# Homes at multiples of 128 bytes for TensorE's operands

## The chip, the core and the metric

The kernel runs on one core of a Trainium2 chip. The metric is the device time of one execution in microseconds (us); the median of three runs of the kernel before is 1080.55 us (1077.29 to 1080.92). SBUF, the on-chip memory from which TensorE reads, has 128 partitions; a tile has the same start address, its home, in each of them. This document gives homes modulo 128 bytes.

## What is computed

Linear attention with an exponential feature map, then two gated MLPs, all in float32:

```python
def phi(x):                                   # x: 4 x 8 heads x 576 x 64
    proj = x @ w_phi                          # 64 -> 128
    proj = proj - max(abs(proj))
    return concat([exp(proj), exp(-proj)])    # 256 features
q_p, k_p = phi(q), phi(k)
kv, z = k_p.T @ v, sum(k_p)                   # per head
x = (q_p @ kv) / (q_p @ z + 1e-6)             # 2304 tokens x 512
x = (silu(x @ w_gate) * (x @ w_val)) @ w_out        # 512 -> 1536 -> 512
x = (sigmoid(x @ w_gate2) * (x @ w_val2)) @ w_out2
```

## The kernel before

**Attention** comes first (to about 190 us). `proj` (line 315) multiplies tiles of q and k by w_phi; every operand is split into a high and a low part (`xh`, `xl`, `w2h`, `w2l`) of type float32r, and three products stand for one. There the moving operand, which streams through the array, is w_phi with 256 columns and the stationary one, which is loaded before, is x with 128. `k_sum` (line 361) sums exp(k) times v; v lies in a tile of four heads with 66 columns each, 64 values and two ones. `turn` (line 383) transposes the subtracted projections of q (`sub`), and `ratio` (line 410) makes numerators and denominators, which go through DRAM; `den_load` (line 430) reads denominators back into a small tile of 18 columns to invert them.

**MLPs** follow. Four passes over the weights (two for each MLP, `hh` 0 to 3) each go over five blocks of tokens, four of 512 and one of 256, and in each over three slots of weights `w0`, `w1`, `w2`: a unit. `product` (line 606) makes the seven products of a Strassen scheme (four in the small block), each as 2 x 2 x 3 matmuls of 256 columns: x is the moving operand, the weights are the stationary one. A full unit has 84 such matmuls, one of the small block 48. ScalarE and VectorE sum and gate the results (lines 626 to 657), and `accumulate` (lines 676 and 678) multiplies by the output weights `o0`, `o1`, `o2`: in passes 0 and 1 the result u of the gate is the moving operand, in passes 2 and 3 the output weights are. Its matmuls are issued between the products of the next unit. While a pass runs, the weights of the next one are loaded, unpacked (lines 158 to 174), stored, loaded again and split (line 198).

**The order.** A planner gives each step a time (`at`), sorts them and issues them in that order; each engine works through its own list. SyncE issues all loads and stores.

**The homes.** Tiles of a pool lie side by side, each rounded up to 32 bytes. Pools on the left grow upwards from the constants: w0, w1 (with o0, o1), `stage`, x0, u, and then `aq` of attention, later replaced by x1. Pools on the right grow downwards from the top of the memory, byte 229344, which is 96 modulo 128: `ap`, `ak`, `ae` of attention, later replaced by w2 (with o2). The pools are opened in lines 111 to 116 and 776 to 777, and `swap` (line 780) replaces them.

Of the kernel before, what the change touches and what calls it, by code (L numbers as in the profile page):

```python
# [9 lines left out]
F32 = mybir.dt.float32  # L10
# [9 lines left out]
P = 128  # L20
# [8 lines left out]
XW = 256  # L29
HW = 512  # L30
VW = D + 2

LEAD = 5
EB = 2
# [70 lines left out]
def body(ctx: ExitStack, tc: tile.TileContext, qT, kT, v, w_phi2, wpk, out):  # L105
# [8 lines left out]
    stage = ctx.enter_context(tc.tile_pool(name="stage", bufs=1))  # L114
# [132 lines left out]
    def plan_attention(ap, ak, ae, aq, t0):  # L247
# [92 lines left out]
        kt, kv, kvz, v1s = {}, {}, {}, {}  # L340

        def load_v(i):
            qd, tt = divmod(i, NT)
            v1s[i] = ak.tile([P, 4, VW], F32, tag="v1", name="v1", bufs=4)
            nc.gpsimd.memset(v1s[i][:, :, D:], 1.0)
            nc.sync.dma_start(
                out=v1s[i][:, :, 0:D],
                in_=v[tt * P:(tt + 1) * P, qd * 256:(qd + 1) * 256]
                .rearrange("p (h d) -> p h d", h=4))

        def k_sum(i, b, r0, r1, first, last):
# [5 lines left out]
            for h in range(4):  # L357
                for s in range(2):
                    c = (h % 2) * 2 + s
                    for u in range(2):  # L360
                        nc.tensor.matmul(  # L361
                            kv[qd, b][h // 2][u * 64:(u + 1) * 64, c * P:c * P + VW],
                            e[r0:r1, h, s, u], v1s[i][r0:r1, h], start=first and c == 0,
                            stop=last and c == 3, skip_group_check=True)

        def kv_keep(qd, b, i):
            if i == 0:
                kvz[qd, b] = aq.tile([P, 4, 2, VW], F32, tag="z", name="z", bufs=2)
            ps = kv[qd, b][i].rearrange("p (h s m) -> p h s m", h=2, s=2)[:, :, :, :VW]
            nc.scalar.copy(kvz[qd, b][:, 2 * i:2 * i + 2], ps)  # L370
# [57 lines left out]
        dw = 4 * S // P  # L428

        def den_load(r, qd, b):  # L430
            r["d"] = stage.tile([P, dw], F32, tag="rc", name="rc", bufs=2)
            nc.sync.dma_start(out=r["d"], in_=den[b][4 * qd:4 * qd + 4]
                              .rearrange("h (p w) -> (h p) w", w=dw))

# [11 lines left out]
        for s, t in enumerate(step):  # L446
            i = s - LEAD
# [14 lines left out]
            if k < n:  # L462
                qd, tt = divmod(k, NT)
                if tt * P % XW == 0:
                    plan_x(kT, "k", qd, tt * P // XW, i)
                at(when(i, 1.5), load_v, k)
                kt[k] = {}
                plan_proj(pe(TP, lambda: None) - TP, kt[k], "k", qd, tt)
# [20 lines left out]
            for qd, g, hp in ratios:  # L489
                g0, m, b = GROUPS[g]  # L490
                e = pe(TR[m == 320], ratio, qd, g, hp)
                at(e + 0.1, ratio_out, qd, g, hp)
                ready["nd"] = e + 0.2
                at(e + 0.8, ratio_store, qd, g, hp)
                if hp == 2 and (g0 + m) % S == 0:
                    r = {}
                    at(e + 4.0, den_load, r, qd, b)
                    at(e + 7.0, den_inv, r)
                    at(e + 7.5, den_store, r, qd, b)
                    ready[b] = e + 7.5  # L500
# [272 lines left out]
    def pool(name, side="left"):  # L773
        return tc.tile_pool(name=name, bufs=1, side=side, reuse_waits="tile")

    aq, ap, ak, ae = pool("aq"), *(pool(name, "right") for name in ("ap", "ak", "ae"))
    aq_, *ap_ = (x.__enter__() for x in (aq, ap, ak, ae))
    T0, ready = plan_attention(*ap_, aq_, 0.0)
# [15 lines left out]
    for hh in range(4):  # L794
        begin.append(t)
        for j, (_, n) in enumerate(BLOCKS):
            if last:
                xprep.append((t, hh, j))
            for p in range(NPAIR):
                r = {}  # L800
# [76 lines left out]
```

## Time and profile before

| | |
|---|---|
| median of three runs | 1080.55 us |
| the profiled execution | 1078.06 us |
| its span, first to last instruction | 1076.0 us |
| granted TensorE clock, mean | 0.99 |
| instructions | 20722 |

The profile is of one execution. PE is TensorE's matmuls and PEld its weight loads, which run beside them; DVE is VectorE, ACT ScalarE, POOL GpSimd and SP SyncE. Matmuls overlap, so that the duration of one is longer than the step from its start to the start of the next; the step is called spacing here. A row names the line, the engine, the operation and the tiles, written one before the arrow; of a matmul's two operands the moving one stands first. Tiles of the same name in attention and in the MLPs (xh, xl, w2h, w2l) are told apart by the line: 315 is attention, 606 the MLPs.

### The profile page before, as it was taken

What the parts mean: (1) busy time and instruction counts of PE and PEld (TensorE: products, weight loads), DVE (VectorE), ACT (ScalarE), POOL (GpSimd) and SP (SyncE); (2) the same over time, 40 slices, a digit from 0 to 9 for tenths busy, and PEclk for the clock granted to TensorE, in tenths of its full rate; (3) what the DMA queues carried; (4) which work ended last, traced back from release to release, by engine and by line L of the source; (5) the groups of instructions that cost most, each with busy time, mean ns of one, the idle gap of its engine ahead of it and who ended that gap; (6) DMA issues with size and microseconds to landing.
All of it is one profiled execution on the core that took longest, in us unless ns stands there. A gap on an engine that the chain in (4) does not pass through costs nothing.

```text
span 1076.0 us, 20722 instructions
## 1 busy us (share of the span) xinstructions
PE 1034.5 (96%) x8344; PEld 928.7 (86%) x8344; DVE 745.5 (69%) x1274; ACT 558.1 (52%) x1006; POOL 126.1 (12%) x109
## 2 busy tenths in 40 slices
PE   7999999997999998999999989999999899999998
PEld 6777776786999888999998889999988799999997
DVE  6988888775766788667757886667487864463433
ACT  5888877643555555535444455455454553332322
POOL 3322330210000014100000132000001230000000
PEclk9999999998999999999999999999999999999999
DMA  7787766648755251445634524155434340331111
GB/s 216 213 243 216 237 190 222 210 117 241 232 172 170 94 187 50 148 136 182 220 120 140 183 99 157 64 190 168 130 97 158 98 147 11 117 119 40 40 40 40
DMA packets 88575, 157.41 MB, mean 146 GB/s; under 512 B 28896, under 2 KB 50592, under 8 KB 88480
## 3 DMA queue, kind: packets, MB, share of 16 engines
q1 hardware_dynamic: 88480, 156.10, 46.2%
q8 instruction: 65, 1.06, 0.4%
q14 instruction: 30, 0.25, 0.1%
HBM read 108.73 MB, written 47.33 MB: 145 GB/s over the span
## 4 chain that ended last, share of the span: by engine, by line
PE 74%; DVE 12%; DMA 8%; ACT 2%; issue 2%; SPq 1%; DVEq 0%; ACTq 0%
PE a L606 22%; PE b L606 16%; PE c L678 7%; PE c L676 5%; PE d L678 5%; PE d L676 5%; PE a L315 5%; PE d L410 4%; PE c L361 3%; DMA rb<-rden 3%; DMA raw<-wpk 2%; DVE xl L198 2%; DVE c L632 1%; PE b L383 1%; DMA o0l<-wfo 1%
## 5 line engine op out<-in xcount | busy, mean ns | idle before, releaser
L644 ACT ACTIVATE c<-c 128x256 f32<-128x256 f32 x96 | 50.4, 525 | 163.9 <-DVE c L632 163.8
L657 DVE TENSOR_TENSOR ul<-c,uh 128x512 fp32r<-128x512 f32 (+1 forms) x120 | 75.1, 635 | 49.5 <-ACT uh L656 48.9
L626 ACT COPY c<-a 128x512 f32<-128x512 f32 x96 | 56.1, 584 | 93.9 <-PE a L606 84.5
L632 DVE TENSOR_TENSOR c<-b,c 128x512 f32<-128x512 f32 x96 | 65.6, 683 | 53.5 <-PE b L606 48.7
L656 ACT CAST uh<-c 128x512 fp32r<-128x512 f32 (+1 forms) x120 | 68.5, 576 | 60.6 <-DVE c L649 52.6
L606 PE MATMUL a<-xh,w2h 128*128 128x256 f32 x288 | 83.1, 288 | 8.7 <-DVE c L632 8.7
L606 PE MATMUL a<-xh,w1h 128*128 128x256 f32 x288 | 81.2, 282 | 8.1 <-DVE c L632 8.1
L606 PE MATMUL a<-xh,w0h 128*128 128x256 f32 x288 | 80.9, 281 | 2.1 <-ACT c L626 1.6
L606 PE MATMUL a<-xh,w2l 128*128 128x256 f32 x288 | 82.6, 287 | 0.0
L606 PE MATMUL a<-xl,w2h 128*128 128x256 f32 x288 | 82.6, 287 | 0.0
L606 PE MATMUL a<-xl,w0h 128*128 128x256 f32 x288 | 80.6, 280 | 0.0
L606 PE MATMUL a<-xh,w1l 128*128 128x256 f32 x288 | 80.4, 279 | 0.0
L606 PE MATMUL a<-xh,w0l 128*128 128x256 f32 x288 | 80.4, 279 | 0.0
L606 PE MATMUL a<-xl,w1h 128*128 128x256 f32 x288 | 80.4, 279 | 0.0
L161 ACT ACTIVATE raw<-raw 128x512 int32<-128x512 uint32 x72 | 48.8, 680 | 60.5 <-DMA raw<-wpk 53.6
L649 DVE TENSOR_TENSOR c<-c 128x256 f32<-128x256 f32 x96 | 56.2, 585 | 27.7 <-ACT c L644 27.1
L198 POOL TENSOR_TENSOR w0l<-s,w0h 128x768 fp32r<-128x768 f32 x6 | 11.3, 1884 | 503.1 <-PE b L606 335.2
L165 DVE TENSOR_SCALAR wcv<-wcv 128x512 f32<-128x512 f32 x72 | 31.4, 437 | 54.6 <-ACT wcv L158 53.6
L606 PEld LDWEIGHTS a<-xh,w2h 128*128 128x128 f32 x288 | 55.4, 193 | 12.1 <-DVE c L632 10.0
L606 PEld LDWEIGHTS a<-xh,w1h 128*128 128x128 f32 x288 | 54.8, 190 | 12.5 <-DVE c L632 10.1
L606 PE MATMUL b<-xh,w2h 128*128 128x256 f32 x224 | 63.2, 282 | 0.0
L606 PE MATMUL b<-xh,w2l 128*128 128x256 f32 x224 | 63.0, 281 | 0.0
(181 smaller groups left out, 3497.4 us busy)
## 6 DMA issues: line engine op xcount, KB each, us to landing
raw<-wpk SPq DMA_DIRECT2D x72, 512.0 KB
b<-xo SPq DMA_DIRECT2D x32, 512.0 KB
wf<-wcv SPq DMA_DIRECT2D x48, 256.0 KB
a<-wf SPq DMA_DIRECT2D x24, 512.0 KB
part<-o SPq DMA_DIRECT2D x17, 512.0 KB
o<-part SPq DMA_DIRECT2D x17, 512.0 KB
wfo<-wcv SPq DMA_DIRECT2D x24, 256.0 KB
x<-kT SPq DMA_DIRECT2D x18, 256.0 KB
```

The costliest lines, as they stand in the source:

```text
L161: nc.scalar.activation(r["lo"].bitcast(I32), r["lo"], AF.Copy, scale=2.0 ** -29)
L315: nc.tensor.matmul(ps[:, i * 256:(i + 1) * 256], x[:, i, o:o + P], w, start=(m == 0 and i == 0), stop=(m == 2 and i == 1), skip_group_chec ...
L410: nc.tensor.matmul(pn[i * w:(i + 1) * w, :m], f, e[:, h, c, :m], start=(c == 0), stop=(c == 1))
L606: nc.tensor.matmul(o, f[:, c], x[:, c], start=k == first and w == 0 and c == 0 and m == 0, stop=c == 1 and m == 2, skip_group_check=True)
L626: anchor["act"] = nc.scalar.copy(part_of(r, d), parts(r, src))
L632: anchor["dve"] = nc.vector.tensor_tensor(out=c, in0=parts(r, "zy x"[d]), in1=c, op=ALU.add)
L644: nc.scalar.activation(o, g, AF.Silu if hh < 2 else AF.Sigmoid)
L649: nc.vector.tensor_tensor(out=o, in0=v, in1=places(r, j, 0, d)[1], op=ALU.mult)
L656: nc.scalar.copy(hi, v)
L657: nc.vector.tensor_tensor(out=lo, in0=v, in1=hi, op=ALU.subtract)
L676: nc.tensor.matmul(ps[:, :n], a[:, k], x, start=st, stop=sp)
L678: nc.tensor.matmul(ps, x[:, k], a, start=st, stop=sp)
```

## The change

Three edits. A tile of 96 bytes is opened first on the right and never used, so that everything on the right lies 96 bytes lower. The two tiles for denominators (`rc`) get 32 columns in place of 18, of which 18 are used; with 128 bytes in place of 96 each, what lies after them on the left moves up by 64. The tile of v gets 288 columns in place of 264, viewed as before.

| tiles | home before | home after |
|---|---|---|
| w0, w1, o0, o1 | 0 | 0 |
| x0, x1 (xh, xl), u (uh, ul) | 64 | 0 |
| w2, o2 | 96 | 0 |
| attention: x's parts, w_phi's parts, exp(k), sub | 96 | 0 |
| v, four buffers | 96, 64, 32, 0 | 0 |
| exp(q) | 64 | 0 |
| z, two buffers | 64, 0 | 0, 64 |

Inside v and z the heads stay 264 bytes apart.

```diff
+LINE = 32
...
         def load_v(i):
             qd, tt = divmod(i, NT)
-            v1s[i] = ak.tile([P, 4, VW], F32, tag="v1", name="v1", bufs=4)
+            v1s[i] = ak.tile([P, 9 * LINE], F32, tag="v1", name="v1", bufs=4)[:, :4 * VW] \
+                .rearrange("p (h d) -> p h d", h=4)
             nc.gpsimd.memset(v1s[i][:, :, D:], 1.0)
...
         def den_load(r, qd, b):
-            r["d"] = stage.tile([P, dw], F32, tag="rc", name="rc", bufs=2)
+            r["d"] = stage.tile([P, LINE], F32, tag="rc", name="rc", bufs=2)[:, :dw]
...
+    edge = ctx.enter_context(pool("edge", "right"))
+    edge.tile([P, 3 * LINE // 4], F32, name="edge")
     aq, ap, ak, ae = pool("aq"), *(pool(name, "right") for name in ("ap", "ak", "ae"))
```

## Rows read from the trace of the kernel before

**Rows 1.** The page: busy us of each engine, share of the span, instructions.

```profile
PE 1034.5 (96%) x8344; PEld 928.7 (86%) x8344; DVE 745.5 (69%) x1274; ACT 558.1 (52%) x1006; POOL 126.1 (12%) x109
```

**Rows 2.** Windows: length, busy us of each engine, granted clock, DMA share, GB/s.

```profile
50.00:100.00 50.00, 49.67 (x668) 38.02 (x667) 41.58 (x72) 40.50 (x85) 15.27 (x20) 1.00 0.79 231
...
186.00:295.00 109.00, 99.20 (x678) 87.95 (x679) 76.50 (x125) 54.41 (x94) 11.60 (x5) 0.95 0.65 199
295.00:412.00 117.00, 113.84 (x840) 106.79 (x840) 86.77 (x155) 64.66 (x111) 8.93 (x5) 1.00 0.46 149
```

**Rows 3.** Waits of TensorE: who for whom, us in total, times, longest.

```profile
PE a L606 <- DVE c L632: 17.3, 8, 3.2
```

**Rows 4.** Chain of waits, 295 to 320 us: start us, us, what.

```profile
306.08 2.72 PE b L606 x24
...
314.25 2.87 PE b L606 x24
```

**Rows 5.** Line 606: count, duration ns min/median/max, first and last start.

```profile
L606 PE MATMUL a<-xh,w1h x288: 276/276/415, 199.7 to 1050.5; 128*128 128x256 f32 x144
...
L606 PE MATMUL a<-xl,w2h x288: 278/282/415, 222.7 to 1064.8; 128*128 128x256 f32 x144
```

**Rows 6.** Chain of waits at the end of the first weight pass.

```profile
397.69 6.68 DMA o0l<-wfo
...
406.42 2.31 DVE xl L198
...
409.89 2.80 DVE w1l L198
...
417.13 2.92 PE a L606 x12
```

**Rows 7.** Timeline of matmuls in attention: start us, us, instruction.

```profile
76.09 0.28 PE L315 MATMUL a<-w2h,xh 128*128 128x256 f32 x1
...
76.69 0.28 PE L315 MATMUL a<-w2h,xl 128*128 128x256 f32 x1
```

**Rows 8.** Line 678 (passes 2 and 3), columns as in rows 5.

```profile
L678 PE MATMUL c<-o1h,uh x40: 388/390/494, 671.8 to 1063.0; 128*128 128x512 f32 x40
...
L678 PE MATMUL c<-o1h,ul x40: 388/392/502, 672.0 to 1063.2; 128*128 128x512 f32 x40
...
L678 PE MATMUL c<-o2h,uh x40: 392/399/402, 687.3 to 1070.0; 128*128 128x512 f32 x40
...
L678 PE MATMUL c<-o2h,ul x40: 392/399/400, 687.6 to 1070.2; 128*128 128x512 f32 x40
```

**Rows 9.** Line 676 (passes 0 and 1), columns as in rows 5.

```profile
L676 PE MATMUL c<-ul,o1h x40: 276/394/504, 225.9 to 627.3; 128*128 128x512 f32 x32, 128*128 128x256 f32 x8
```

**Rows 10.** Chain of waits, 725 to 755 us.

```profile
730.64 2.83 PE b L606 x24
...
741.88 2.83 PE b L606 x24
```

**Rows 11.** Groups of 420 to 610, then 860 to 1050 us: busy, mean ns.

```profile
L606 PE MATMUL b<-xl,w0h 128*128 128x256 f32 x56 | 15.5, 276 | 0.0
...
L606 PE MATMUL b<-xl,w0h 128*128 128x256 f32 x52 | 14.5, 279 | 0.0
```

**Rows 12.** Chain of waits: sums over two v buffers.

```profile
67.54 2.17 PE c L361 x64
...
111.66 2.17 PE c L361 x64
```

**Rows 13.** Groups of ScalarE, shapes apart: busy us, mean ns, idle before.

```profile
L197 ACT CAST w0h<-a 128x1024 fp32r<-128x1024 f32 x8 | 8.5, 1058 | 0.9 <-DVE a L216 0.9
...
L197 ACT CAST w2h<-a 128x1024 fp32r<-128x1024 f32 x8 | 8.4, 1050 | 0.3 <-DVE a L216 0.2
```

**Rows 14.** Timeline of weight loads in attention, columns as in rows 7.

```profile
76.09 0.19 PEld L315 LDWEIGHTS a<-w2l,xh 128*128 128x128 f32 x1
```

## The prediction

> **What bounds the kernel now.** I began with the busy times: TensorE is at 96% of the span, VectorE at 69%, ScalarE at 52% [rows 1]. Then the stages: from 50 to 100 us (attention) TensorE is busy for 49.67 of 50 us, and from 295 to 412 us for 113.84 of 117 us, which is the level of every later stage; only 186 to 295 us, where the first weights and activations of the MoE layers arrive, is at 91% [rows 2]. The waits of TensorE confirm it: the longest sum is 17.3 us in 8 waits, product's matmuls for VectorE's line 632 [rows 3]. So nearly every nanosecond between two matmuls counts, and the question is whether the homes of the operands set any of them.
>
> The change adds no instruction, DMA or wait: the edge tile is never touched, the values and denominators keep their shapes inside wider tiles, and every engine's program keeps its order. Only addresses move. So what has to be read is the spacing of matmuls by the home of their operands. I write "moving/stationary" for the two homes modulo 128 bytes: product (line 606) is 64/0 for w0 and w1 and 64/96 for w2; the projection (line 315) is 96/96; the output sums are 64/0 and 64/96 (line 676), 0/64 and 96/64 (line 678).
>
> Unbroken stretches of 24 products give the spacing best. 64/0 takes 2.72 us at 306 us, 113.3 ns each; 64/96 takes 2.87 us at 314 us, 119.6 ns each [rows 4]; the difference of 0.15 us is 6.25 ns a matmul. [...] The medians over the whole run say it again, 276 against 282 ns [rows 5]. The profile's duration holds some 163 ns beside the spacing (276 less 113), so differences of durations are differences of spacing.
>
> **The change part by part.** All terms are against the profiled execution, 1078.06 us (span 1076.0 and 2.06 around it).
>
> Edge tile, w2's products. Three groups (xh by w2h, xl by w2h, xh by w2l) of 288 and 224 make 1536 matmuls with weights from w2. If home 96 is what slows them and 0 gives w0's spacing, they save 1536 x 6.25 = 9.6 us. Not all of it is on the path. Near the end of each weight pass a chain of other work decides: the load of o0l (6.68 us), VectorE's splits (2.31 and 2.80 us) and the sum at line 632 fill 397.7 to 417.1 us before product goes on [rows 6]. A whole w2 unit (84 matmuls) lies under it, in three passes, and one more under the early waits of 186 to 295 us; there the gain only lengthens a wait. On the path remain 1536 - 4 x 84 = 1200, or 7.5 us. If home 96 costs nothing, the term is 0.
>
> Edge tile, projection. Both operands are at 96: from 76.09 to 76.69 us stand five spacings of 120 ns [rows 7]. 432 x (120 - 113.3) = 2.9 us; attention is bound by TensorE, and its end starts the normalisation for which the first MoE blocks wait, so the gain is kept. I count 2.6, leaving out the start, where DMA sets the pace; the lower end is 0 here too.
>
> Edge tile, w2's output weights. As the moving operand (line 678) o2 shows 399 and 399 ns where o1 shows 390 and 392 [rows 8]: 9 + 7 ns, each for 72 matmuls (40 into c and 32 into d), is 1.1 us. As the stationary one (line 676) I take 0, since its neighbour with o1 already stands at 394 ns [rows 9].
>
> Products of w0 and w1 in the second half. The 64/0 pair that took 2.72 us takes 2.83 us at 730 and 741 us, in units that follow w2 and o2 [rows 10], and the means of w0 rise from 276 to 279 ns [rows 11]. I found no operand that differs; the slower rhythm seems to be handed on by a misaligned neighbour. Taken at about 1.5 ns on the 1536 products of w0 and w1 in that half (w1's means rise less), 2.3 us is at stake; between 0 and 2.3 I take 1.5.
>
> Denominator tiles widened: x and u move from 64 to 0. This is the unknown term, since no row before has 0/0. The nearest rows are a pair that differs in which side is at 0: with 0/64 (o1 moving) a 512-column matmul lasts 390 and 392 ns, with 64/0 (o1 stationary) 394 ns as median [rows 8, 9]. A moving operand at 0 is no clear gain there, so I take 0. [...] The upper end is the third rival.
>
> Values padded. v's four homes were 96, 64, 32 and 0; two runs of 64 matmuls from different buffers take 2.17 us each [rows 12], so its own home costs nothing, and padding only brings the subtracted tiles below it to 0; they are stationary operands of the transposes, whose spacing no row shows at another home: 0. z's two buffers only swap their homes: 0. The writers of all moved tiles are nearest to ScalarE's casts, 1058 ns into w0 and 1050 into w2 [rows 13]: homes 0 and 96 alike, so 0.
>
> Sum: 7.5 + 2.6 + 1.1 + 1.5 = 12.7 us, 1078.06 - 12.7 = 1065.4 us. The median of the three runs is 1080.55, 2.5 above the profiled execution; from there it would be 1067.9. I put 1066, and 1060 to 1072 as this case's own range.
>
> **The rivals.**
> Even 64 costs, and 0/0 is faster than any row. [...] Against it: wide matmuls with a moving operand at 0 hardly stand below those at 64 [rows 8, 9]. [...]
>
> The home is not the cause. w2, the projection's tiles and o2 have in common that they lie at the high end of the memory, not only that they start at 96. If that place slows them, a shift by 96 bytes changes nothing: 1078 us. For it: nothing in the trace separates the two, and the homes of v make no difference [rows 12]. Against it: 96/96, 64/96 and 96/64 lie in different phases beside different neighbours, and all are slower. [...]
>
> Equal homes collide (slower). The next weight load begins with the current matmul: at 76.09 us both start [rows 7, 14]. If their reads disturb each other when both begin at the same place within 128 bytes, then 64/0 was the good arrangement, and the change makes all pairs equal. The only equal pair before, 96/96, takes 120 ns [rows 7]; at 6.25 ns the 3072 products of w0 and w1 lose 19.2 us, the wide matmuls of o0 and o1 go to o2's durations, 144 x 16 ns = 2.3 us, and w2 gains nothing: 1078 + 22 = 1100 us. It decides as soon as the equal start, and not the distance from a multiple of 128, is what counts. Against it: 64/96 and 96/64 are unequal and slow as well.
>
> **How the numbers follow.** Forecast 0.43, even lower 0.26, no effect 0.17, collision 0.14. Less than 0.5% (5.4 us) can't be told from no change here. The first two are faster, except for 0.02 in which the chains of the weight passes take most of the gain; no effect is the same but for 0.02 on either side. So faster 0.69, same 0.15, slower 0.16. The range goes from 1032, which takes in most of the lower rival, to 1082, no effect with the spread of the runs.
>
> **What would show it.** After the change 24 products of w2 should take 2.72 us and not 2.87, five projections 0.57 us and not 0.60, o2's matmuls 390 to 394 ns, and the stretches at 730 and 741 us 2.72 us. If w0 and w1 fall below 113 ns as well, the first rival holds; if w2 stays at 119, the second; if w0 rises to 119, the third. The waits for line 632 should grow by about 0.5 us in each of three weight passes. I'd be wrong in another way if the spacings fall as said and waits grow by as much.

## The result, and the profile after

The change makes the kernel slower. The median is 1089.75 us (1083.23 to 1092.42, 7 runs) against 1080.44 us (1075.84 to 1081.54, 7 runs), a ratio of 1.0085 with a 95% interval of 1.0062 to 1.0109. The forecast was 1066 and its range 1032 to 1082: wrong in sign. The rival in which equal homes collide names what happened.

The page of the kernel after, busy us of each engine, answers [rows 1]: VectorE and ScalarE are where they were, TensorE has 14.0 us more, nearly all that the span has gained (14.4, from 1076.0 to 1090.4). The granted clock is 0.990 and 0.992 in the mean of the two executions, so the clock is not the reason. The profiled execution of the kernel before (1078.06 us) lies 2.4 us below the median of its seven runs and that of the kernel after (1092.42) 2.7 above its own, so 14.4 us between the profiles stand for 9.3 between the medians.

```profile
PE 1048.5 (96%) x8344; PEld 945.0 (87%) x8344; DVE 747.4 (69%) x1274; ACT 558.9 (51%) x1006; POOL 127.2 (12%) x109
```

The chain of waits of the kernel after, 300 to 320 us (start, us, what), answers [rows 4]. The first row is 24 products of w1, the second of w2. Both take 2.88 us, 120.0 ns each: w2 was not brought down to w0 and w1, w0 and w1 were brought up to it.

```profile
308.17 2.88 PE b L609 x24
...
316.81 2.88 PE b L609 x24
```

The small block of pass 2, 725 to 765 us, answers [rows 10]. Here too there is now one spacing for all.

```profile
740.43 2.88 PE b L609 x24
...
751.67 2.88 PE b L609 x24
```

Line 609, which is line 606 of before, over the whole run (count, duration ns min/median/max), answers [rows 5]: 276 and 282 have become 283 and 283.

```profile
L609 PE MATMUL a<-xh,w1h x288: 277/283/415, 203.1 to 1065.0; 128*128 128x256 f32 x144
...
L609 PE MATMUL a<-xl,w2h x288: 282/283/420, 224.2 to 1079.4; 128*128 128x256 f32 x144
```

The projection in attention, timeline of matmuls, answers [rows 7]: from 77.50 to 78.10 us again five spacings of 120 ns. Moving both operands from 96 to 0 did nothing.

```profile
77.50 0.28 PE L317 MATMUL a<-w2l,xh 128*128 128x256 f32 x1
...
78.10 0.28 PE L317 MATMUL a<-w2h,xh 128*128 128x256 f32 x1
```

The output matmuls, line 681, answer [rows 8], and line 679 answers [rows 9]: o2 falls from 399 to 396 and 395 ns, but o1 rises from 390 and 392 to 396 and 397. With the stationary o1 in passes 0 and 1 the median is unchanged.

```profile
L681 PE MATMUL c<-o1h,uh x40: 392/396/495, 680.8 to 1077.5; 128*128 128x512 f32 x40
...
L681 PE MATMUL c<-o1h,ul x40: 389/397/499, 681.1 to 1077.7; 128*128 128x512 f32 x40
...
L681 PE MATMUL c<-o2h,uh x40: 389/396/396, 696.4 to 1084.4; 128*128 128x512 f32 x40
...
L681 PE MATMUL c<-o2h,ul x40: 389/395/398, 696.6 to 1084.6; 128*128 128x512 f32 x40
```

```profile
L679 PE MATMUL c<-ul,o1h x40: 283/394/504, 227.3 to 636.1; 128*128 128x512 f32 x32, 128*128 128x256 f32 x8
```

Waits of TensorE (us, times, longest) answer [rows 3]: nothing new appeared there.

```profile
PE a L609 <- DVE c L635: 17.6, 7, 3.5
```

Where the 14.4 us between the two profiled executions lie can be added up from the steps between the starts of matmuls in the MLPs, a step over 140 ns (products) or 260 ns (outputs) being counted as a wait for what it has beyond. Products 537.5 to 553.4 us (+15.9), outputs 301.7 to 299.8 (-1.9), waits 41.7 to 39.1 (-2.6), and the first product starts 3.0 us later (185.9 to 188.9). This last part lies within the scatter: over the executions profiled below the start is between 184.3 and 189.8 us, in no relation to the homes that shows. The loss is in the products, and there in w0 and w1: their mean step goes from 114.5 to 119.7 ns, 5.2 ns on 3072 products or 16 us, while that of w2 stays (119.6 and 119.7).

### The profile page after: what moved, and what is told of

It reads as the page before. It is cut to its first block, busy times and chain, and to the rows that moved or that the text cites. A ratio compares the mean times of both kernels' runs of the same rounds, so it can differ in the third digit from the quotient of the medians.

```text
span 1090.4 us, 20722 instructions
## 1 busy us (share of the span) xinstructions
PE 1048.5 (96%) x8344; PEld 945.0 (87%) x8344; DVE 747.4 (69%) x1274; ACT 558.9 (51%) x1006; POOL 127.2 (12%) x109
## 4 chain that ended last, share of the span: by engine, by line
PE 72%; DVE 11%; DMA 11%; ACT 2%; issue 2%; SPq 1%; POOL 0%; DVEq 0%; ACTq 0%; POOLq 0%
PE a L609 22%; PE b L609 16%; PE c L681 7%; PE d L681 5%; PE c L679 5%; PE d L679 5%; PE a L317 4%; PE d L413 4%; PE c L364 3%; DMA rb<-rden 3%; DMA raw<-wpk 2%; DVE xl L200 2%; DMA o0l<-wfo 1%; DVE c L635 1%; PE b L386 1%
## 5 line engine op out<-in xcount | busy, mean ns | idle before, releaser
L609 PEld LDWEIGHTS a<-xh,w1h 128*128 128x128 f32 x288 | 55.6, 193 | 11.8 <-DVE c L635 9.7
L200 DVE TENSOR_TENSOR xl<-b,xh 128x1024 fp32r<-128x1024 f32 (+1 forms) x40 | 50.6, 1265 | 21.5 <-ACT xh L199 21.4
L609 PE MATMUL b<-xh,w1h 128*128 128x256 f32 x224 | 63.6, 284 | 0.0
```

Of the source, the lines that this page charges most:

```text
L200: eng.tensor_tensor(out=lo, in0=src, in1=hi, op=ALU.subtract)
L609: nc.tensor.matmul(o, f[:, c], x[:, c], start=k == first and w == 0 and c == 0 and m == 0, stop=c == 1 and m == 2, skip_group_check=True)
```

## Experiments

In all of them the distance of a pair is the stationary home less the moving home, modulo 128. Before, product had distance 64 (w0, w1) and 32 (w2); after, 0.

**One part undone: the denominator tiles.** Only x and u go back to 64.

```diff
-            r["d"] = stage.tile([P, LINE], F32, tag="rc", name="rc", bufs=2)[:, :dw]
+            r["d"] = stage.tile([P, dw], F32, tag="rc", name="rc", bufs=2)
```

> The changed kernel with the denominator tiles back at 18 columns: x and u return to home 64, the weights of all three slots and o2 stay at 0, so every product is 64/0. Theory 'distance' (what counts is the stationary home less the moving home, modulo 128: 64 is fast, 0 and 32 are slow): all three slots at 113.3 ns, w2's 24 products 2.72 us, time about 9 us below the kernel before, near 1071 us. Theory 'the shifted right side costs' (the loss comes from the edge tile or from the padded values): w0 and w1 at 113, but the time stays above 1080 us.

Median 1073.77 us, 0.9953 (0.9928 to 0.9979) of the kernel before. The chain of waits shows the small block of pass 1, w1 at 525 and w2 at 533 us, at 113.3 ns each; w2 has lost its handicap. In the same run other stretches take 117.8 ns though their homes are the same, as at 584 us: distance 64 has two rhythms, one with steps of 113 and 114 ns, the other of 117 to 119. That is one reason why the gain by the ratio is 5 us and not 9. The profiled execution is also the slowest of the seven (1078.73 us), no faster than the profiled execution of before (1078.06): its products take 6.7 us less (530.8), but its waits 5.0 us more (46.7), and the first product starts 3.9 us later.

```profile
525.32 2.72 PE b L609 x24
...
533.48 2.72 PE b L609 x24
...
584.89 2.83 PE a L609 x24
```

**The other part undone: the edge tile.** w2 and o2 go back to 96, x and u stay at 0.

```diff
-    edge = ctx.enter_context(pool("edge", "right"))
-    edge.tile([P, 3 * LINE // 4], F32, name="edge")
```

> The changed kernel without the edge tile: x and u at 0, w0 and w1 at 0, w2 and o2 back at 96. w0 and w1 have distance 0 and stay at 120 ns by either theory. w2 is now 0/96, distance 96, a pair that no run has shown: theory 'distance' with a charge that depends on how far apart the two reads are, either way round, expects 119.6 as at distance 32; a weight load that trails the matmul by a few ns would make 96 differ from 32 and could give 113. Time 1090 us in the first case, near 1081 in the second.

Median 1085.19 us, 1.0063 (1.0037 to 1.0088). The small block of pass 1, in the order w0, w1, w2: 119.6, 120.0 and 117.5 ns. Distance 96 differs from 32 (119.6 before) but is not fast. So the widened denominator tiles cost time without the edge tile as well (v is padded in both of these runs), and the edge tile without them is what helps.

```profile
518.14 2.87 PE b L609 x24
...
529.47 2.88 PE b L609 x24
...
538.11 2.82 PE b L609 x24
```

**Six distances in a run, twice.** Each tile of product begins at its own place inside a wider tile (the third run of this kind, further down, uses the same helper).

```diff
+    def at_home(pool, n, off, tag, name):
+        return pool.tile([P, n + LINE * (off > 0)], R32, tag=tag, name=name)[:, off:off + n]
...
+                xs[hh, j] = [at_home(pools[f"x{k}"], 14 * NQ, XO_[k], x, x)
+                             .rearrange("p (c q n) -> p c q n", c=2, q=7) for x in ("xh", "xl")]
```

> The changed kernel with the homes of the product's operands shifted inside wider tiles: x0 at 0 and x1 at 64; w0 at 0, w1 at 32, w2 at 96. Six pairs: with x0 the distances (stationary less moving) are 0, 32 and 96, with x1 64, 96 and 32. Theory 'distance': the two pairs of distance 32 agree (about 119.6 ns), the two of distance 96 agree, 0 gives 120 and 64 gives 113.3. Theory 'absolute home' (x at 64 is good and x at 0 is bad in itself): all units on x1 stand below all units on x0.

> As the scan before, with w0 at 16, w1 at 48 and w2 at 80: with x0 (home 0) the distances are 16, 48 and 80, with x1 (home 64) 80, 112 and 16. Theory 'distance': the two pairs of 16 agree, and so do the two of 80; 48 and 80, nearest to 64, are the fast ones (113 ns or below) and 16 and 112 the slow ones (about 120). Theory 'absolute home': x1 is faster than x0 whatever the weights' home.

The small block of pass 2, on x0 (home 0), in the order w0, w1, w2; first distances 0, 32 and 96, then 16, 48 and 80.

```profile
734.20 2.87 PE b L613 x24
...
745.43 2.85 PE b L613 x24
...
753.91 2.83 PE b L613 x24
```

```profile
729.40 2.84 PE b L613 x24
...
740.55 2.87 PE b L613 x24
...
749.02 2.83 PE b L613 x24
```

These are 119.6, 118.8 and 117.9 ns, then 118.3, 119.6 and 117.9. On x1, at home 64, the median of the units' means is 117.4 (distance 64), 117.2 (96), 118.3 (32), then 119.1 (80), 117.2 (112) and 118.8 (16). A moving operand at 64 is not good in itself: in the second run w0 and w2 are slower on x1 than on x0, where their medians are 118.0 (16) and 118.1 (80). Pairs of one distance agree only within 1 ns (80: 118.1 and 119.1), and all distances but 0 lie within 2, so these runs alone don't prove the rule. What I had wrong is the neighbourhood of 64: 48 and 80 are as slow as the rest, and distance 64 itself came out at 117.4, in its slow rhythm, in every unit. Each gives one time, 1083.11 and 1079.46 us.

**The mirror, and equal homes that are not 0.** Both start from a pad of 64 bytes below w0 and an edge tile of 32 bytes; the mirror has the narrow denominator tiles as well.

```diff
+    ctx.enter_context(tc.tile_pool(name="low", bufs=1)).tile([P, LINE // 2], F32, name="low")
...
-    edge.tile([P, 3 * LINE // 4], F32, name="edge")
+    edge.tile([P, LINE // 4], F32, name="edge")
```

> The mirror of the run with narrow denominator tiles: a pad of 64 bytes below w0, an edge tile of 32 in place of 96 bytes and the denominator tiles at 18 columns put all weights and output weights at 64 and x and u at 0. No operand of product has the homes it had before, the distance is 64 everywhere. Theory 'distance': products at 113.3 ns, with stretches at 117.8 as before, time 0.3 to 0.7% below the kernel before. Theory 'absolute home' (x or u at 0 is slow in itself): about 120 ns and the changed kernel's 1090 us.

> Pad of 64 bytes below w0, edge tile of 32 bytes, wide denominator tiles: every operand of the MLPs at 64, so all pairs are equal but no home is a multiple of 128. Theory 'distance': 120 ns in all units, as 0/0. Theory 'absolute home' (64 is good for the moving operand): 113 ns.

The mirror (0/64): median 1074.44 us, 0.9968 (0.9951 to 0.9985), with both rhythms of distance 64, here 117.9 ns in pass 1 and 113.3 in pass 2.

```profile
524.65 2.83 PE b L610 x24
...
731.21 2.72 PE b L610 x24
```

All at 64 (64/64): means of 119.4 to 120.0 ns in every unit, as in the changed kernel (119.5 to 120.0), and one time of 1089.08 us.

```profile
527.01 2.88 PE b L610 x24
...
535.65 2.88 PE b L610 x24
```

0/64 behaves as 64/0 and 64/64 as 0/0. So what tells the fast case from the slow one is the distance between the two operands, not the home of either. The distance doesn't fix the spacing alone: at 64 there are two rhythms, and 32 took 119.6 ns in the kernel before but 118.3 and 118.8 in the scan.

**What picks the rhythm at distance 64: u at 0.** Narrow denominator tiles, u shifted by 64 bytes, so that only the output matmuls have distance 0.

> Narrow denominator tiles (x at 64, all weights at 0: product has distance 64 everywhere), but u shifted to 0 inside wider tiles, so that the output matmuls between the products are 0/0. Theory 'handed on' (at distance 64 there are two rhythms, 113.3 and 117.8 ns, and which one runs is inherited from the matmuls before; output matmuls at distance 0 start the slow one): products at about 117.7 ns nearly everywhere, time 1083 to 1090 us. Theory 'each pair for itself': products at 113.3 ns for the most part, as with u at 64, and the time of that run, about 1074 us.

Median 1076.75 us, 0.9995 (0.9978 to 1.0012). The small blocks of passes 1 and 2:

```profile
518.33 2.72 PE b L613 x24
...
736.38 2.83 PE b L613 x24
```

Half a hit, in the rhythm and not in the time. In passes 2 and 3 nearly all products (93% of the steps are above 115.5 ns) take the slow rhythm, in passes 0 and 1 only 24%. Each such share is of one execution: in the four kernels of this section with all products and outputs at distance 64 (narrow denominator tiles, the mirror, the shifted projection, the edge tile alone) it is 18 to 52% in passes 0 and 1 and 27 to 49% in passes 2 and 3. The matmuls between seem to decide something, but not by distance 0 alone.

**Distance 64 in the projection.**

```diff
-        w2h = ap.tile([P, 2 * F], R32, name="w2h")
-        w2l = ap.tile([P, 2 * F], R32, name="w2l")
+        w2h, w2l = (ap.tile([P, 2 * F + LINE], R32, name=x)[:, LINE // 2:LINE // 2 + 2 * F]
+                    for x in ("w2h", "w2l"))
```

> Narrow denominator tiles and w_phi's parts shifted by 64 bytes, so that the projection of attention has distance 64 as well. Theory 'distance': within a group of 12 projections the spacing falls from 120 to 113 to 118 ns, 1 to 3 us in all on the path; with the 5 us of the run with narrow denominator tiles the time is 0.5 to 0.9% below the kernel before. If the short groups of attention always start in the slow rhythm, the gain there is 1 us or less.

Median 1074.34 us, 0.9958 (0.9939 to 0.9978), the same as without the shift. Of the three kinds of projection one clearly falls, from 282 to 279 ns, and the mean step only from 119.0 to 117.9. Distance 64 brings little here; that the fast rhythm doesn't start in groups of 6 or 12 is a guess.

```profile
L317 PE MATMUL a<-w2l,xh x144: 276/279/582, 5.1 to 184.7; 128*128 128x256 f32 x144
```

**Output weights at 96.** Narrow denominator tiles; first o2, then all three output weights begin 96 bytes into wider tiles.

> Narrow denominator tiles (x and u at 64, weights at 0, products at distance 64 everywhere), but o2, the output weights of the third slot, shifted to 96 as in the kernel before. Theory 'handed on, with a reset': at distance 64 either rhythm, 113.3 or 117.8 ns, goes on until another distance breaks it, and after such a break the products fall into the fast one; o2's output matmuls then reset it in every third unit. Expected: long stretches of 117.8 ns vanish, products at 113.3 to 114.4 nearly everywhere, some 3 to 7 us less than with narrow denominator tiles alone, 0.6 to 1.1% below the kernel before. Theory 'rhythm by chance at waits of TensorE': as many slow stretches as without the shift, 0.3 to 0.5% below.

> As relock_o2, with all three output weights at 96, so that each unit's output matmuls are at another distance than 64. Theory 'handed on, with a reset': products at 113.3 to 114.4 ns in all units, less what the output matmuls lose themselves (1 to 2 ns on 1224, up to 2 us): 0.6 to 1.1% below the kernel before, about as relock_o2. Theory 'rhythm by chance at waits': slow stretches remain, and the time is that of narrow denominator tiles or 2 us more.

Medians 1076.91 and 1076.92 us, 0.9978 (0.9960 to 0.9995) and 0.9985 (0.9970 to 1.0000). The reset doesn't work as I thought. Products are slow in 17% and 16% of their steps in passes 0 and 1 but in 85% and 89% in passes 2 and 3. In the second of the two runs:

```profile
520.52 2.73 PE b L613 x24
...
739.26 2.83 PE b L613 x24
```

**Period and width of the good place.** w1 at 128 (distance 64 modulo 128, 192 modulo 256) and w2 at 8 (distance 72).

> Narrow denominator tiles, x and u at 64, o at 0; w0 at 0 (distance 64), w1 at 128 (distance 64 modulo 128, but 192 modulo 256), w2 at 8 (distance 72). If 128 bytes is the period, w1 shows the same two rhythms as w0 (113.3 and 117.8 ns); if the period is 256 or more, w1 has a spacing of its own, near 120. w2 tells how wide the good place is: 113.3 if 8 bytes don't matter, 117 to 119 if they do.

The small block of pass 3, w0, w1, w2: 113.8, 113.3 and 117.9 ns. A shift by 128 bytes keeps the fast rhythm here; 8 bytes off, no unit reaches it (unit means 117.8 to 119.8). In other units w1, which comes before w2 and after w0, stands at 117.2 (in two at 119.0), so it is not always fast either. One time, 1076.37 us.

```profile
948.10 2.73 PE b L613 x24
...
959.09 2.72 PE b L613 x24
...
967.43 2.83 PE b L613 x24
```

**The edge tile alone, on the kernel before.**

> The kernel before with the edge tile alone: w2 and o2 at 0, x and u at 64, v unpadded. Against the changed kernel with narrow denominator tiles only v's padding is gone (v and the subtracted tiles off their homes). If padding does nothing, both have one time, 0.3 to 0.6% below the kernel before; if v's home matters in attention, the time differs by more than 2 us.

Median 1071.12 us, 0.9942 (0.9918 to 0.9965): this beats both kernels, the one before by 6 us and the changed one, by the two ratios, by some 15. Its interval overlaps with that of the run with narrow denominator tiles, so no effect of padding v shows. The gain is still only some half of the 12.7 us forecast: the mean step of w2 falls from 119.6 to 115.1 ns and not to 113.3, that of w0 and w1 rises from 114.5 to 115.0, and together the products gain 5.2 us (532.3). The rows are w1 and w2 of the small block in pass 1, and a slow stretch of pass 2.

```profile
519.42 2.72 PE b L606 x24
...
527.59 2.72 PE b L606 x24
...
745.95 2.83 PE b L606 x24
```

**All output matmuls at distance 32.** Output weights at 96 in passes 0 and 1, at 32 in passes 2 and 3.

> Narrow denominator tiles, products at distance 64, and the output weights at 96 in passes 0 and 1 and at 32 in passes 2 and 3, so that all output matmuls have distance 32 (in the run with all of them at 96 it was 32 in the first two passes, where the fast rhythm prevailed, and 96 in the last two, where the slow one did). Theory 'the distance of the output matmuls picks the rhythm': products at 113.3 to 114.4 ns in all four passes, 0.5 to 1% below the kernel before. Theory 'passes 2 and 3 fall into the slow rhythm by their form, with the output weights as the moving operand': 117.8 ns there as in the run with all at 96, 0.1 to 0.2% below.

Median 1076.54 us, 0.9999 (0.9985 to 1.0013). Products are slow in 69% of their steps in passes 2 and 3 and in 18% in passes 0 and 1, at the same distance, so the distance of the output matmuls alone does not pick the rhythm. With outputs at distance 64 the share in passes 2 and 3 was 27 to 49%, so their form alone doesn't seem to either. What picks it stays open.

## Why the prediction was wrong, point by point

**What bounds the kernel**: right. TensorE's steps were the bound, and the span grew by 14.4 us with 15.9 us more in the products. The homes that I worked out agree with every run, and the count of instructions is the same.

**The steps that failed** are the edge tile's first term, "home 96 is what slows them and 0 gives w0's spacing", and the denominator tiles' "A moving operand at 0 is no clear gain there, so I take 0". Both give a home to one operand and ask what it costs. The runs show that the pair counts: 0/0 and 64/64 at 120 ns, 64/0 and 0/64 at 113.3 or 117.8, the other distances at 117 to 120. So w2 at 0 was worth something only while x stayed at 64, and the same diff took that away. Measured against the working: product 15.9 us longer in place of 7.5 and 1.5 us shorter, the latter for w0 and w1 in the second half. The term put at 0 is the one that cost most, 16 us on w0 and w1. Even without that loss the sum was too large: 12.7 us were given, and the edge tile alone brings 6.3 (3.8 to 8.9) by its ratio.

That the reads of a matmul and those of the next weight load get in each other's way is a possible reason, but no run here shows the reads themselves. What the runs show is that the same matmuls and loads, moved against each other by 64 bytes, go from 113.3 ns (24 products of w1 in 2.72 us, narrow denominator tiles, at 525 us) to 120.0 (2.88 us in the kernel after, at 308 us).

The low end of the range, 1032 us, rests on a guess of mine that 0/0 could stay below 113.3 ns. No run shows such a spacing: 0/0 took 119.5 to 120.0 ns, and the lowest mean of a unit in any run here is 113.3 ns.

**Projection**: 2.6 us were expected, 0 came (mean step 119.1 ns before and after): 96/96 and 0/0 are both distance 0. **Output weights of w2**: 1.1 us were expected; o2 fell by 3 and 4 ns where 9 and 7 were expected, o1 rose, and all output matmuls together gained 1.9 us. **Products in the second half**: I saw the rhythm of 117.8 ns and guessed that a misaligned neighbour hands it on; it is there with w2 and o2 at 0 too (2.83 us at 584 us, narrow denominator tiles). **Values padded**: 0 predicted, and no effect shows.

**The rivals.** Equal homes collide had the condition, the place and the sign, and 0.14 of the chance; its mechanism, reads that disturb each other, is neither shown nor excluded. Its price of 22 us was too high for the 9.3 us between the medians (6.7 to 11.8 by the interval), and for the profiled products: w0 and w1 were not all at 113.3 ns before, and the output matmuls, for which I added 2.3 us, lost nothing. The row that should have moved me was the only equal pair, 96/96 at 120 ns. I set against it that 64/96 and 96/64 are slow too, which is true but speaks only against "unequal is fast", not against "64 apart is fast". The rivals of still lower spacing and of no effect are out: no unit of product has a mean below 113.3 ns in any run, and homes do act.

## What to carry to other kernels

Where float32r matmuls of some 256 columns run back to back, try the homes of the stationary and the moving operand 64 bytes apart modulo 128 (here 113.3 or 117.8 ns a product, against 119.4 to 120.0 at equal homes), and read the result from the spacing of a stretch of equal matmuls. It is no guarantee: the projection gained little by it (a mean step of 117.9 ns after 119.0), and on x1 of the first scan all units at that distance kept the slow rhythm (117.4 ns). Before taking one operand's home for the cause, write down both homes of every pair in the trace; a "good" home can be good only against its partner: x at 64 went with 113.3 or 117.8 ns beside weights at 0 and with 119.4 to 120.0 beside weights at 64.

## What the hardware showed that I had not expected

At distance 64 the stream of products has two steady rhythms, 113.3 and 117.8 ns, which go on for tens of microseconds in one execution with the same addresses: with narrow denominator tiles the stretches of 24 on the chain of waits take 117.9 ns each from 888 to 978 us and 114.6, in the fast one, from 990 to 1051. In the same run the spacing was 113.3 ns at 540 us and 117.9 at 585; between them lies a wait of line 679 for line 660, over at 573.6 us. 8 bytes off that distance the fast rhythm is gone, in one execution (unit means of 117.8 to 119.8 ns). The 512-column output matmuls of passes 2 and 3 hardly tell distance 0 from 64: their mean step is 230.1 ns in the kernel after and 231.2 with u at 0, 229.3 to 229.9 ns in the four kernels with products and outputs at 64, but 233.0 at distance 96 and 234.7 at 32.
